# Gating products spread between the stages of a delta-rule attention loop

## Chip, cores and metric

The kernel runs on one core of a Trainium2 chip. The metric is the device time of one execution in microseconds. Lower is better. [...]

## The reference, cut to what matters

Three layers follow one another, all in float32, with B = 4, H = 8 heads of D = 48, S = 768, model width 384, inner width 1024:

```python
# 1: delta-rule attention, a recurrence over the 768 tokens of 32 (batch, head) units
k_n = k / (norm(k) + 1e-6)
for t in range(S):
    y[:, :, t] = einsum('bhd,bhde->bhe', q[:, :, t], state)
    v_old = einsum('bhde,bhd->bhe', state, kt)
    state = state + bt * einsum('bhd,bhe->bhde', kt, vt - v_old)
# 2: gating layer on x = y as (batch, token, 384)
h = gelu(x @ w_in);  u, v = h[..., :512], h[..., 512:]
v_n = layernorm(v) * g_ln
v_s = einsum('ts,bsd->btd', w_sg, v_n) + b_sg
x = x + (u * v_s) @ w_out
# 3: squared-relu layer with a shift by one token and a sigmoid gate
k = maximum(xk @ w_k, 0); out = sigmoid(xr @ w_r) * (k * k @ w_v)
```

## The kernel before, in words

The attention is done in chunks of 64 tokens: 12 chunks s, two of them a group g, six groups. In each chunk the 32 units fall into two halves o. Five stages make one chunk and half: st_rq (state times keys, and keys times keys and queries, into PSUM; then the sum `r` of line 466 on DVE, or of line 464 on ACT in group 0; then copies on ACT and masks on GpSimd), st_d (the solved 32 x 32 inverses times r; copied by ACT as u1), st_n (the coupling of a chunk's two 32-token blocks; copied by ACT), st_s (the state's update; copied) and st_y (the outputs; copied, and stored into xT by SP's queue). Each stage is a Python generator: its first piece issues the matmuls, the second the copies or the sum, the third, of st_rq alone, the negated copies and the masks. The matmuls of a stage are small (32 to 64 columns; lines 489, 492, 512, 525, 540, 554).

A group needs two things before its chunks: Gram blocks (`gram`, lines 328 and 330, eight halves of 32 pairs of weight load and matmul, in four jobs of two halves) and triangular inverses that `solver` makes on DVE in some hundred small steps over about a group's time; when they are there, `couple` (line 448, 64 pairs, called for k = 0 and 1) multiplies them on TensorE.

Meanwhile the gating layer is prepared. `fill(n)` issues the products x @ w_in of earlier tokens (lines 624 and 676) worth n, a 512-column product counting 1 and a 256-column one 0.5. Such products come in units of nine; each group of tokens brings 72. If none is ready, `fill` issues warming products on a zero tile (`keep_warm`, line 715) in their place. Before a gating unit ends, gelu on ACT must empty its PSUM bank. The weights come as float64 bit pairs: `narrow` turns a block into a rounded part and a rest with DVE, ACT and GpSimd, and `scratch` stores both to DRAM; these jobs are started by `tick`.

The order on TensorE, ACT, DVE and GpSimd is the order in which this Python code issues. The loop has 12 x 4 runs; `run` issues one slot's stages (st_n and st_rq in turn with st_d, st_s, st_y), and then three points (`tick`): at each, due calls of `after(n, f)` (n points later), DVE's background steps of a budget of 1.62 (1.05 times that in group 0), at some points a Gram block; and at the end `fill(n)`, where n comes from a planned slot of 5.315 us less the run's costs by the table COST, at 0.235 us for a product. `used` carries what was over or left. Eight runs, 24 points, are a group. From point 125 on, one step a point of `early_items` prepares the mixing of the second layer (`begin_early`: fetches of w_sg into `stw`, their splits, the ring of v). A DMA that is issued by `nc.sync` stands in SP's one queue; it waits there for what it reads or overwrites, and later ones behind it.

Behind the loop, x_split, the gating units of the last group, mixing products (line 935) and the splits of w_sg's second half are issued in turn, then projection and the third layer.

Of the kernel before, what the change touches and what calls it, by code (L numbers as in the profile page):

```python
# [7 lines left out]
F32 = mybir.dt.float32  # L8
# [9 lines left out]
DM = 384  # L18
FF = 1024
HF = 512  # L20
P = 128
# [10 lines left out]
SV = 60  # L32
B0 = 1.05
PRE = 0.8
GRAM0 = 17
SOLVE0 = 1
RUN = (3, 2, 3)
SUMS = (0,)
EVERY = 6
LATE = 100  # L40
PUT = 2
JLAG = 2
BUDGET = 1.62
SLOT = 5.315
GSTEP = 2
LAGC = 2
JS = 18
NT_ = (3, 3, 3)
LNW = 1
# [5 lines left out]
COST = dict(rq=1.05, d=0.8, n=0.8, s=0.85, y=1.1)  # L55
# [26 lines left out]
def fused_kernel(  # L82
# [17 lines left out]
    nc = tc.nc  # L100
# [87 lines left out]
    def scratch(dram, name, nblk, n, cw=CW, pool=stg):  # L188

        d = dp.tile([nblk, P, 2, n], F32, name=name + "_d")  # L190

        def job(i, j):
            parts = []
            yield from narrow(dram, i, j, None, None, cw, pool, parts=parts)

            def put():
                nc.sync.dma_start(out=d[i, :, :, j:j + cw], in_=parts[0])

            yield PUT, put

        return d[:, :, 0], d[:, :, 1], [lambda i=i, j=j: job(i, j) for i in range(nblk) for j in range(0, n, cw)]
# [38 lines left out]
    with ExitStack() as at:  # L240
# [112 lines left out]
        def solver(g):  # L353
# [46 lines left out]
            for dst in (0, 1):  # L400
                for p in range(2):
                    o = 16 * p
# [33 lines left out]
            DTs[g] = DT  # L436
            yield 1.14
            for k in range(2):
                after(LAGC + k, lambda k=k: couple(g, k))

        def couple(g, k):

            w = bank()[:].rearrange("p a (b c) -> p (a b) c", c=32)
            GL, DT, u0 = GLs[g], DTs[g], NPR * k
            for u in range(u0, u0 + NPR):
                for h in range(2):
                    r = 64 * (1 - h)
                    T.matmul(w[r:r + 32, u - u0, :], lhsT=GL[r + 32:r + 64, u, :],  # L448
                             rhs=DT[r + 32:r + 64, u, :], start=True, stop=True)
            for r in (64, 0):  # L450
                A.activation(GL[r:r + 32, u0:u0 + NPR], w[r:r + 32], AF.Copy)
            used[0] += 1.4
            joined.add(2 * g + k)

        def scale_v(s):
# [125 lines left out]

        units, grams, opened, owed, splits, used = [], [], [[], None], [0], [], [0]
        spent = [0, 0, 0]
        later, vstat, streams, point = [], {}, [], [0, 0]

        def after(n, f):
            later.append((point[0] + n, f))
# [164 lines left out]
                    running[:] = [r for r in running if r[1] is not e[1]]  # L754
            debt[0] = min(t, 0) * (point[1] > 0)

        running, debt = [], [0]
        jobs = in_jobs + jobs
        n_jobs = len(jobs)

# [61 lines left out]
        def tick():  # L822
            g, n = divmod(point[0], 24)
            point[1] = min(g, 1) + 1
            gg, nn = divmod(point[0] - GRAM0, 24)
            if nn == 0 and 0 <= gg and gg + 2 < NG:
                grams.extend(gram(gg + 2))
            if n == 0 and g + 1 < NG:
                streams.append([point[0] + SOLVE0, solver(g + 1), "solve"])
            late = point[0] >= LATE  # L830
            if point[0] < LASTP and jobs and len(running) < RUN[1 + late] and n % (2 if late else EVERY) == 0:
                start_job(LJ5 if late else LJ)
            background(BUDGET * (B0 if g == 0 else 1))
            while len(jobs) > n_rest and len(running) < RUN[0]:
                start_job()
            if grams and (point[0] - GRAM0) % GSTEP == 0:
                for _, f in grams.pop(0):
                    f()
                used[0] += 1.1
            point[0] += 1  # L840

        def run(*todo):
            bodies = [f(s, o) for f, s, o in todo]
            used[0] += sum(COST[f.__name__[3:]] for f, _, _ in todo)
            for _ in range(3):
                for b in bodies:
                    next(b, None)
            for _ in range(3):
                tick()
                if early_items and point[0] >= FROM:  # L850
                    early_items.pop(0)()
            n = min(max((SLOT - used[0]) / 0.235, 3), 14)
            used[0] += n * 0.235 - SLOT
            fill(n)

        ring, rb, wsl, early_items = {}, [], [[], []], []

# [13 lines left out]
        def begin_early():  # L871
            vst = [slot(G0[c + 1], [P, HF]) for c in range(4)]
            st = {0: fetch_pair(slot(W0[2], [P, 2, DM]), 0),
                  1: fetch_pair(stg.tile([P, 2, DM], F32, name="stw", bufs=1), 1)}
            for c in range(4):
                nc.sync.dma_start(out=vst[c], in_=vn_d[0, c])

            def ws(c):
                i, k = divmod(c, 2)
                if k == 0:  # L880
                    t = [slot(x, [P, 2, DM], F32R) for x in W0[2 * i:2 * i + 2]]
                    wsl[0].extend((t[0][:, e], t[1][:, e]) for e in range(2))
                split(A, V, st[i][:, k], *wsl[0][c])
                if c == 3:
                    st[2] = fetch_pair(stg.tile([P, 2, DM], F32, name="stw", bufs=1), 2)

            for x in (0, 1, 10, 2, 11, 3, 12, 13, 4, 5):
                early_items.append((lambda c=x: ws(c)) if x < 10 else
                                   (lambda c=x - 10: to_ring(0, c, vst[c])))

        for s in range(12):
# [297 lines left out]
```

## Time and profile before

| | us |
|---|---|
| median of three runs | 777.8 |
| lowest and highest of them | 776.1, 784.21 |
| the profiled execution, its own time | 785.01 |
| its span from first to last instruction | 783.3 |
| mean granted clock of TensorE in it | 0.961 |

The times of the rows below come from the profiled execution and are counted from the start of its span. The attention loop is the stretch from 56.8 to 345.9 us.

### The profile page before, as it was taken

What the parts mean: (1) busy time and instruction counts of PE and PEld (TensorE: products, weight loads), DVE (VectorE), ACT (ScalarE), POOL (GpSimd) and SP (SyncE); (2) the same over time, 40 slices, a digit from 0 to 9 for tenths busy, and PEclk for the clock granted to TensorE, in tenths of its full rate; (3) what the DMA queues carried; (4) which work ended last, traced back from release to release, by engine and by line L of the source; (5) the groups of instructions that cost most, each with busy time, mean ns of one, the idle gap of its engine ahead of it and who ended that gap; (6) DMA issues with size and microseconds to landing.
All of it is one profiled execution on the core that took longest, in us unless ns stands there. A gap on an engine that the chain in (4) does not pass through costs nothing.

```text
span 783.3 us, 25096 instructions
## 1 busy us (share of the span) xinstructions
PE 717.5 (92%) x10898; PEld 658.0 (84%) x10898; DVE 504.7 (64%) x1071; ACT 373.2 (48%) x752; POOL 199.9 (26%) x246
## 2 busy tenths in 40 slices
PE   3479989899998999798889979999999999999998
PEld 3335768788887887686879969999999999999997
DVE  6997779779597895622265967269664564564441
ACT  2234566566766767753333332128463463452330
POOL 3143335344363564520216351201000000000000
PEclk9979999899799999999989989999999999999999
DMA  8312346365566647538367554228000000000000
GB/s 240 79 62 67 112 94 190 104 187 168 130 175 175 189 142 199 180 106 223 122 228 237 180 163 146 75 87 222 21 11 31 11 21 31 11 21 31 11 22 31
DMA packets 82159, 88.76 MB, mean 113 GB/s; under 512 B 24704, under 2 KB 65024, under 8 KB 82048
## 3 DMA queue, kind: packets, MB, share of 16 engines
q1 hardware_dynamic: 76816, 77.92, 33.8%
q0 software_dynamic: 4800, 9.04, 4.2%
q8 instruction: 85, 1.39, 0.8%
q10 hardware_dynamic: 432, 0.20, 0.1%
q14 instruction: 26, 0.21, 0.1%
HBM read 56.60 MB, written 25.82 MB: 105 GB/s over the span
## 4 chain that ended last, share of the span: by engine, by line
PE 75%; DMA 7%; DVE 7%; issue 3%; POOL 3%; ACT 2%; SPq 2%; POOLq 0%; DVEq 0%
PE ms L146 35%; PE ms L676 7%; PE ms L935 6%; PE ms L624 6%; PE ms L715 4%; PE ms L554 3%; PE rk L512 3%; PE rk L489 2%; PE rk L525 2%; PE sps L540 2%; PE ms L448 2%; PE ms L328 2%; DVE sg L350 1%; DMA raw<-in_w_r_dram 1%; POOL na L172 1%
## 5 line engine op out<-in xcount | busy, mean ns | idle before, releaser
L146 PE MATMUL ms<-wvh,sl 128*128 128x384 f32 x192 | 64.6, 336 | 0.0
L146 PE MATMUL ms<-wvl,sh 128*128 128x384 f32 x192 | 64.5, 336 | 0.0
L146 PE MATMUL ms<-wvh,sh 128*128 128x384 f32 x192 | 64.5, 336 | 0.0
L146 PE MATMUL ms<-xm_hi,sw0h 128*128 128x384 f32 x192 | 64.2, 335 | 0.0
L146 PE MATMUL ms<-xm_hi,sw0l 128*128 128x384 f32 x192 | 64.2, 334 | 0.0
L146 PE MATMUL ms<-xm_lo,sw0h 128*128 128x384 f32 x192 | 64.2, 334 | 0.0
L172 POOL TENSOR_TENSOR na<-na,raw 128x256 int32<-128x256 int32 (+2 forms) x43 | 38.3, 890 | 86.1 <-DVE na L170 80.4
L118 DVE TENSOR_TENSOR sl<-sg,sh 128x384 fp32r<-128x384 f32 x64 | 35.6, 557 | 30.3 <-ACT sh L115 30.2
L935 PE MATMUL ms<-sw0h,g 128*128 128x384 f32 x192 | 50.4, 336 | 2.1 <-DVE g L118 2.1
L115 ACT ACTIVATE sh<-sg 128x384 fp32r<-128x384 f32 x64 | 33.5, 524 | 36.3 <-DVE sg L1109 36.3
L935 PE MATMUL ms<-ws1h,g 128*128 128x384 f32 x192 | 49.9, 334 | 0.0
L676 PE MATMUL ms<-xh,wiu_hi 128*128 128x256 f32 x144 | 41.0, 303 | 6.9 <-ACT v L633 6.9
L1125 DVE TENSOR_TENSOR sg<-sg,ms 128x384 f32<-128x384 f32 x24 | 13.3, 554 | 46.2 <-PE ms L146 46.2
L1109 DVE TENSOR_TENSOR sg<-sg 128x384 f32<-128x384 f32 x64 | 35.3, 552 | 11.5 <-ACT sg L1108 11.4
L350 DVE TENSOR_TENSOR sg<-sg,Yt 128x512 f32<-128x512 f32 (+10 forms) x78 | 41.5, 532 | 1.6
L1108 ACT ACTIVATE sg<-ms 128x384 f32<-128x384 f32 x64 | 30.8, 481 | 24.2 <-PE ms L146 23.9
L676 PE MATMUL ms<-xl,wiu_hi 128*128 128x256 f32 x144 | 40.0, 297 | 2.4 <-issue 2.4
L115 ACT ACTIVATE gh<-w 128x384 fp32r<-128x384 f32 x32 | 16.6, 524 | 53.5 <-DVE w L1022 53.5
L676 PE MATMUL ms<-xh,wiu_lo 128*128 128x256 f32 x144 | 40.4, 299 | 0.1
L146 PE MATMUL ms<-gh,wo_hi 128*128 128x384 f32 x96 | 35.2, 366 | 5.7 <-ACT gh L115 5.7
L505 POOL TENSOR_SCALAR_AFFINE_SELECT SQ<-SQ 64x512 f32<-64x512 f32 x36 | 26.9, 746 | 48.0 <-ACT SQ L504 41.1
L676 PEld LDWEIGHTS ms<-xh,wiu_hi 128*128 128x128 f32 x144 | 27.7, 201 | 13.1 <-ACT v L633 8.2
(236 smaller groups left out, 2244.9 us busy)
## 6 DMA issues: line engine op xcount, KB each, us to landing
u_d<-ug SPq DMA_DIRECT2D x24, 256.0 KB, 4.1
u<-u_d SPq DMA_DIRECT2D x16, 384.0 KB, 5.5
vn_d<-v SPq DMA_DIRECT2D x22, 256.0 KB, 3.8
vk<-in_vk_dram SPq DMA_DIRECT2D x24, 192.0 KB, 3.9
vk<-in_vk_dram SPq DMA_DIRECT2D x12, 384.0 KB, 4.9
out_dram<-sg SPq DMA_DIRECT2D x24, 192.0 KB, 1.9
SQ<-in_q_d_dram SPq DMA_DIRECT2D x36, 96.0 KB, 3.6
xT<-yst SPq DMA_DIRECT2D x23, 144.0 KB, 3.8
```

The costliest lines, as they stand in the source:

```text
L115: A.activation(hi, src, AF.Copy)
L118: eng_lo.tensor_tensor(lo, src, hi.bitcast(F32), op=ALU.subtract)
L146: T.matmul(pt, lhsT=a, rhs=b, start=(i == 0), stop=(i == n - 1))
L172: G.tensor_tensor(a.bitcast(I32), a.bitcast(I32), w_lo.bitcast(I32), op=ALU.add)
L350: V.tensor_tensor(tv, vw(a_t, a_off, a_dims), vw(b_t, b_off, b_dims), op=ALU.mult)
L505: G.affine_select(out=pt, in_=pt, pattern=[[0, 8], [1, C]], compare_op=ALU.is_gt, fill=0.0, base=0, channel_multiplier=-1)
L624: T.matmul(vstat[g, b], lhsT=a[:, c], rhs=w[:, c], start=first, stop=last)
L676: T.matmul(vstat["u"][:, 2 * P * d:2 * P * d + 2 * P], lhsT=w[:, c, ds_], rhs=a[:, c].rearrange("p b t -> p (b t)"), start=first, stop=last)
L715: T.matmul(o, lhsT=warm, rhs=vw(warm, 0, [(0, 4), (1, P)]), start=True, stop=True)
L935: T.matmul(pt[:, :DM], lhsT=v[:, ds_], rhs=w, start=(c == 0 and i == 0), stop=(c == 5 and i == 2))
L1108: A.activation(r, pt[:, :DM], AF.Relu)
L1109: V.tensor_tensor(r, r, r, op=ALU.mult)
```

## The change

The order in which TensorE gets its work inside the loop is made anew. `run` now issues for each stage its matmuls and its second piece and then a share of the run's products (`fill(gap)`); the third pieces, the points, and after them the calls in `batches`, each followed by another share. Gram blocks and couples go to `batches`: a block as two halves. Blocks stand at points 13, 18, 21 and 23 of a group (before: 17, 19, 21, 23), couples 2 and 8 points behind the solver's end (before: 2 and 3). The run's number of products is planned ahead: `need` counts the stages, 1.1 for each Gram point in the run and 1.4 for a run that begins at point 0 or 6, whether or not there is a block or couple; between 3 and 15 products (before 3 to 14), with at most 1 us carried on. The stores of rounded blocks (column width below 384: those of w_out and w_k, 20 of them) are issued by GpSimd in place of SP, one point after the split in place of two. Jobs start at points 0, 5, 10, 15, 20 of a group in place of 0, 6, 12, 18, and every second point from 110 on in place of 100. The third fetch of w_sg in `begin_early` is issued two points later, and the two splits that read it two points later.

```diff
@@ -32,18 +32,17 @@
 SV = 60
 B0 = 1.05
 PRE = 0.8
-GRAM0 = 17
+GRAMS = (13, 18, 21, 23)
 SOLVE0 = 1
 RUN = (3, 2, 3)
 SUMS = (0,)
-EVERY = 6
-LATE = 100
-PUT = 2
+EVERY = 5
+LATE = 110
+PUT = 1
 JLAG = 2
 BUDGET = 1.62
 SLOT = 5.315
-GSTEP = 2
-LAGC = 2
+LAGC = (2, 8)
 JS = 18
 NT_ = (3, 3, 3)
 LNW = 1
@@ -194,7 +193,7 @@
             yield from narrow(dram, i, j, None, None, cw, pool, parts=parts)
 
             def put():
-                nc.sync.dma_start(out=d[i, :, :, j:j + cw], in_=parts[0])
+                (G if cw < DM else nc.sync).dma_start(out=d[i, :, :, j:j + cw], in_=parts[0])
 
             yield PUT, put
 
@@ -436,7 +435,10 @@
             DTs[g] = DT
             yield 1.14
             for k in range(2):
-                after(LAGC + k, lambda k=k: couple(g, k))
+                after(LAGC[k], lambda k=k: join(g, k))
+
+        def join(g, k):
+            batches.append(lambda: couple(g, k))
 
         def couple(g, k):
 
@@ -449,7 +451,6 @@
                              rhs=DT[r + 32:r + 64, u, :], start=True, stop=True)
             for r in (64, 0):
                 A.activation(GL[r:r + 32, u0:u0 + NPR], w[r:r + 32], AF.Copy)
-            used[0] += 1.4
             joined.add(2 * g + k)
 
         def scale_v(s):
@@ -581,7 +582,7 @@
 
 
 
-        units, grams, opened, owed, splits, used = [], [], [[], None], [0], [], [0]
+        units, grams, opened, owed, splits, spare = [], [], [[], None], [0], [], [0]
         spent = [0, 0, 0]
         later, vstat, streams, point = [], {}, [], [0, 0]
 
@@ -754,7 +755,7 @@
                     running[:] = [r for r in running if r[1] is not e[1]]
             debt[0] = min(t, 0) * (point[1] > 0)
 
-        running, debt = [], [0]
+        running, debt, batches = [], [0], []
         jobs = in_jobs + jobs
         n_jobs = len(jobs)
 
@@ -822,7 +823,7 @@
         def tick():
             g, n = divmod(point[0], 24)
             point[1] = min(g, 1) + 1
-            gg, nn = divmod(point[0] - GRAM0, 24)
+            gg, nn = divmod(point[0] - GRAMS[0], 24)
             if nn == 0 and 0 <= gg and gg + 2 < NG:
                 grams.extend(gram(gg + 2))
             if n == 0 and g + 1 < NG:
@@ -833,25 +834,33 @@
             background(BUDGET * (B0 if g == 0 else 1))
             while len(jobs) > n_rest and len(running) < RUN[0]:
                 start_job()
-            if grams and (point[0] - GRAM0) % GSTEP == 0:
-                for _, f in grams.pop(0):
-                    f()
-                used[0] += 1.1
+            if grams and point[0] % 24 in GRAMS:
+                batches.extend(f for _, f in grams.pop(0))
             point[0] += 1
 
         def run(*todo):
-            bodies = [f(s, o) for f, s, o in todo]
-            used[0] += sum(COST[f.__name__[3:]] for f, _, _ in todo)
-            for _ in range(3):
-                for b in bodies:
-                    next(b, None)
+            n = point[0] % 24
+            plan = sum(k in GRAMS for k in range(n, n + 3)), n in (0, 6)
+            need = sum(COST[f.__name__[3:]] for f, _, _ in todo) + 1.1 * plan[0] + 1.4 * plan[1]
+            gap = min(max((SLOT - need + spare[0]) / 0.235, 3), 15)
+            spare[0] = min(spare[0] + SLOT - need - 0.235 * gap, 1)
+            gap /= len(todo) + 2 * plan[0] + plan[1] + (n < 3 and not todo)
+            bodies = []
+            for f, s, o in todo:
+                b = f(s, o)
+                next(b, None)
+                next(b, None)
+                bodies.append(b)
+                fill(gap)
+            for b in bodies:
+                next(b, None)
             for _ in range(3):
                 tick()
                 if early_items and point[0] >= FROM:
                     early_items.pop(0)()
-            n = min(max((SLOT - used[0]) / 0.235, 3), 14)
-            used[0] += n * 0.235 - SLOT
-            fill(n)
+            while batches:
+                batches.pop(0)()
+                fill(gap)
 
         ring, rb, wsl, early_items = {}, [], [[], []], []
 
@@ -882,10 +891,10 @@
                     wsl[0].extend((t[0][:, e], t[1][:, e]) for e in range(2))
                 split(A, V, st[i][:, k], *wsl[0][c])
                 if c == 3:
-                    st[2] = fetch_pair(stg.tile([P, 2, DM], F32, name="stw", bufs=1), 2)
-
-            for x in (0, 1, 10, 2, 11, 3, 12, 13, 4, 5):
-                early_items.append((lambda c=x: ws(c)) if x < 10 else
+                    after(2, lambda: st.update({2: fetch_pair(stg.tile([P, 2, DM], F32, name="stw", bufs=1), 2)}))
+
+            for x in (0, 1, 10, 2, 11, 3, 12, 13, 20, 20, 4, 5):
+                early_items.append((lambda c=x: ws(c)) if x < 10 else (lambda: None) if x == 20 else
                                    (lambda c=x - 10: to_ring(0, c, vst[c])))
 
         for s in range(12):
```

## Rows read from the trace of the kernel before

**Rows 1.** The page: busy share and instructions of each engine; instruction queue (packets, MB).

```profile
PE 717.5 (92%) x10898; PEld 658.0 (84%) x10898; DVE 504.7 (64%) x1071; ACT 373.2 (48%) x752; POOL 199.9 (26%) x246
...
q8 instruction: 85, 1.39, 0.8%
```

**Rows 2.** Windows, groups 0 to 5, behind: width, PE PEld DVE ACT POOL busy, clock, DMA.

```profile
56.80:96.70 39.90, 39.44 (x1078) 25.59 (x1077) 30.87 (x73) 20.27 (x45) 12.88 (x16) 1.00 0.28 84
96.70:148.40 51.70, 46.74 (x1377) 39.21 (x1376) 43.38 (x99) 33.18 (x66) 22.30 (x27) 0.93 0.51 136
148.40:198.80 50.40, 45.98 (x1390) 40.03 (x1388) 39.59 (x95) 33.95 (x67) 21.92 (x29) 0.97 0.58 162
198.80:249.80 51.00, 47.87 (x1390) 42.69 (x1389) 41.35 (x94) 33.79 (x67) 22.18 (x28) 0.90 0.59 165
249.80:296.30 46.50, 46.47 (x1163) 40.75 (x1162) 39.28 (x92) 31.58 (x60) 25.85 (x29) 0.93 0.58 162
296.30:345.90 49.60, 44.93 (x1115) 37.32 (x1114) 23.40 (x44) 34.91 (x68) 22.73 (x33) 0.93 0.58 166
345.90:400.00 54.10, 44.62 (x304) 41.05 (x303) 13.19 (x25) 18.83 (x32) 6.91 (x12) 0.97 0.62 173
```

**Rows 3.** Chain of waits in group 1, an even stretch: start us, us, what.

```profile
113.02 3.40 PE ms L624 x14
116.41 0.81 PE rk L512 x64
...
119.16 1.12 PE ms L624 x4
...
122.18 0.80 PE rk L525 x32
...
124.08 2.59 PE ms L676 x20
...
131.37 1.81 PE ms L624 x7
```

**Rows 4.** Chain of waits in groups 4 and 5: a couple, warming products.

```profile
260.64 1.13 PE ms L448 x64
...
300.14 2.05 PE ms L715 x9
```

**Rows 5.** Chain of waits in groups 1 and 3: pauses and what stands around.

```profile
98.34 0.46 issue
...
99.48 1.70 PE ms L448 x100
101.18 2.27 issue
...
138.38 3.29 PE ms L624 x7
...
246.84 2.41 issue
```

**Rows 6.** Windows, a stretch of half clock; columns as in rows 2.

```profile
199.80:210.00 10.20, 10.20 (x304) 9.59 (x301) 7.71 (x34) 6.53 (x13) 3.64 (x8) 0.50 0.39 107
```

**Rows 7.** Timeline of TensorE, group 5 and behind: start, us, line, [idle before, releaser].

```profile
330.20 1.98 PE L554 MATMUL ms<-SQ 128*64 128x64 f32 x32 [2.52 <-ACT ug L680]
...
364.36 0.96 PE L624 MATMUL ms<-wiv_hi,xh 128*128 128x512 f32 x3 [0.48 <-ACT xh L115]
...
371.96 0.61 PE L676 MATMUL ms<-xh,wiu_hi 128*128 128x256 f32 x3 [3.22 <-ACT v L633]
```

**Rows 8.** Waits of SP's queue, whole span: us in total, times, longest.

```profile
SPq L197 <- POOL raw L118: 72.9, 22, 8.7
```

**Rows 9.** Timeline of DVE in group 1: start, us, line.

```profile
125.33 0.54 DVE L466 TENSOR_TENSOR r<-vk,rk 128x384 f32<-128x384 f32 x1
```

**Rows 10.** Issues of DMAs by GpSimd, two lines: ns min/median/max, first and last start.

```profile
L207 POOL DMA_DIRECT2D wo_hi<-wo_d x1: 1003/1003/1003, 349.6 to 349.6; - x1
...
L1064 POOL DMA_DIRECT2D sw0l<-wk_d x3: 537/537/650, 501.9 to 516.6; - x3
```

## Prediction

> **What bounds the kernel now.** I read first the page's busy shares, then a table of windows with one row for each group of the attention loop, then the chain of waits, piece by piece, inside that loop. TensorE is busy 92% of the span [rows 1]. The loop (56.8 to 345.9 us, six groups of eight runs) takes 289.1 us [rows 2], and in it nearly every piece of the chain is a TensorE piece that begins where the last one ended. So the loop lasts as long as what is put on TensorE's queue, plus the places where that queue stops or runs slowly.
>
> What a group should take follows from pieces in an undisturbed stretch [rows 3]: 14 gating products take 3.40 us (0.243 each), st_d, st_s and st_y together 2.75 us (116.41 to 119.16), st_n 0.80 and st_rq 1.10 (122.98 to 124.08), and one Gram block (64 pairs of weight load and matmul) 1.02 us, the time from the end of st_y at 130.34 to the first product at 131.37. A couple takes 1.13 us [rows 4]. Eight runs are 4 x 1.90 + 4 x 2.75 = 18.6; four Gram blocks 4.1; two couples 2.3; and the planner's 72 products 17.5: together 42.5 us. Groups 1, 2 and 3 took 51.7, 50.4 and 51.0 [rows 2], 25.6 us more in all.
>
> Where that goes can be read off. **Stops**: at 98.34, 101.18 and 246.84 TensorE stands still for 0.46, 2.27 and 2.41 us and the chain calls it "issue", so nothing that the profile shows held it [rows 5]. Between the first two stops the engine ran the last 27 pairs of st_rq and 100 of the couple, 127 pairs. One instruction transfer carries 256 instructions (2 x 10898 instructions in 85 transfers [rows 1]), which is 128 pairs: the stops sit where such a block ends. They come in or just behind long strings of small matmuls (Gram, couples). The loop has nine "issue" stops over 0.4 us, from 82.20 to 246.84, three of them shown: 0.42, 0.46, 2.27, 1.98, 1.14, 0.63, 1.19, 0.72 and 2.41, together 11.2 us. [...]
>
> **The change part by part.** (1) *Spreading.* No pair is added or taken away: a Gram block becomes two halves of 32 pairs with products behind each, and products stand behind each stage instead of at the run's end. The two couples of a group, which fell into one run in groups 1 to 3, are six points apart; one of four Gram blocks moves from the run at point 15 to the one at 12. But the run at point 21 keeps two blocks behind st_d, st_s, st_y, 256 small pairs with the least number of products, 3, among them. Price per block when the queue is dry: from 98.80 to 103.45, 4.65 us for 128 pairs, the upper bound; the lower bound is that a block costs nothing beyond its own matmuls. In the three runs from point 18 to point 2 the kernel before issues about 656 pairs in 16 us by plan; less one block of lead, 528 / 128 x 4.65 = 19.2, so 3.2 us of stop per group (seen: 3 to 5). With a couple less it is some 596 pairs: 17.0, so 1.0 us per group. I take 4 us of stops left of 11.2, and about a quarter of the half clock, 3 of 12.2 us: a gain of 16. [...] The first run has 15 warming products where it had 10, some 1 us more.
>
> (2) *Number of products.* Both planners' arithmetic (5.315 less the stages' costs, over 0.235) gives the same total through group 3, 306 and 304. After it the new one charges Gram blocks at points 13, 18, 21 and 23 of groups 4 and 5, where there are none, and drops their share of the products: 180 planned before, 120 after. 60 x 0.243 = 14.6 us leave TensorE's loop. 19 of these were warming products, as the one row of nine shows [rows 4] with two more of five: pure gain, 4.6 us. The other 41 are real and move behind the loop. There they meet the time up to 364.36, when the last group's last block comes to its products [rows 7], already filled with mixing, and three pauses, of which the first, 3.22 us, is shown [rows 7], with 2.25 and 0.67 behind it, in which banks wait for gelus on ACT. I take it that 3 us of their 10 are absorbed: +7 behind the loop (bounds 0 and 10).
>
> (3) *What is late next.* DVE is busy 43.4, 39.6, 41.4 and 39.3 us in groups 1 to 4 [rows 2], with a rounding more per group now (5 starts in 24 points, not 4), for which I allow up to 2 us. TensorE's 42.5 is thus just where DVE ends as well, and in group 4, where TensorE would need only 34 (18.6 + 2.3 + 53 x 0.243), DVE sets the end. In group 5 it is ACT, 34.9 us. So I take 45.5, 44, 44.5, 41.5 and 41.5 for groups 1 to 5 and 39.5 for group 0: 256.5 against 289.1. These values hold the gains of (1) and (2) inside the loop, capped by the other engines; for half clock that the caps' own short waits bring back I add 3.
>
> (4) *Less cover behind st_rq.* Its sum on DVE (line 466) must be there before st_d of the next run. Before, all products of the run, 3.4 us, lay between; now a half of them, with a couple or Gram block in groups 0 to 3 some 2.2 to 2.9 us, but in four runs of groups 4 and 5 only 2.5 products, 0.6 us. The sum takes 0.54 us and started as late as 1.25 us after the products it reads ended at 124.08 [rows 9]. So 18 runs hide it, four wait up to 1.3 us: at most 5 us, in groups that other engines bound anyway; nothing added.
>
> (5) *Stores by GpSimd.* 20 stores of rounded blocks leave SP's queue. SP stood 72.9 us for GpSimd's last step of such blocks, up to 8.7 at a time [rows 8], with loads of keys and queries and stores of gating results queued behind. In group 5 a gelu on ACT, whose buffer waits for such a store, made st_y wait 2.52 [rows 7]; that wait and the half clock after it should go (in group 5's 41.5). On GpSimd each issue costs 0.54 to 1.0 us by its issues behind the loop [rows 10], 11 to 20 us over a loop in which it was busy 128 of 289 us [rows 2]; queued behind are the roundings' sums, on which ACT waits, and st_rq's masks, needed three runs later. I take nothing for it and up to 5 us in the range.
>
> (6) *Third gating fetch two points later, its splits two steps later, late roundings from 110, stores one point earlier*: SP no longer stands for that fetch's buffer; at most 2 us either way, taken as nothing.
>
> The sum is made on the profiled execution (785.0 us, span 783.3): 289.1 - 256.5 = 32.6, less 3 of returned half clock, less 7 behind the loop: 22.6, so 762. The runs' median is 777.8, and 22.6 from that gives 755. Part of the 7 us between the two must be stops and half clock that the change takes away in either case; I take the middle, **758 us**.
>
> **The rivals.** *Blocks still run dry.* At 21 to 24 points four blocks' worth of small pairs remain with few products. If a refill costs the 4.65 us throughout and half of the half clock stays, (1) brings 8 instead of 16: 767. For: three products do not fill 256 pairs. Against: neighbours are now lighter.
>
> *The stops are no refills.* Then they have a cause that the order of the products does not touch, a pause of TensorE's own queue that comes wherever the long strings stand, and they and the half clock stay. Only the 19 warming products, the wait of 2.52 and 3 us of clock around it are gained, 4.6 + 2.5 + 3, so 768. The distance of 127 pairs between two stops [rows 5] speaks against it; that a stop in group 3 [rows 5] falls among products and not in a string speaks for it. [...]
>
> *All of it comes through.* Postponed products fit wholly into the pauses and the other engines follow: 7 + 3 more, 745 to 748.
>
> *DVE late for st_d (slower than before).* If DVE, with no slack left, runs behind by over 1.7 us at each of the 22 sums, the cover of (4) is gone in every run: 22 waits of 1.2 us are 26 us, TensorE falls to half clock in their wake (5 us), and the postponed products (10) come without relief: 41 against a gain of 32.6, 786. It decides from about 1 us of wait per run on. For: groups at 95 to 100% DVE. Against: at 125.33 the sum, 1.25 late, ended at 125.87 [rows 9], 1.6 us before 14 products behind st_rq would (124.08 + 3.4).
>
> **How the numbers follow.** Forecast 0.5 (750 to 766), blocks still dry 0.18, no refills 0.1, all of it 0.14, DVE late 0.08. A measurement of this kernel tells about 1% (the runs lie from 776.1 to 784.2). Faster by over 1% (under 770): forecast, all of it and most of the two at 767 and 768, 0.78; within 1% 0.14; slower 0.08. The range that leaves out no more than 2 in 10 reaches from 743 to 775.
>
> **What would show it.** Right: groups 1 to 3 near 44.5 us, "issue" in the chain under 5 us of the loop, granted clock 0.97 or more in each group, DVE over 90% busy in groups 1 to 4, no SP wait for a store of a rounded block in the loop, three warming rows at the end of group 4 gone; some 41 products more behind the loop and that part 5 to 10 us longer. Wrong: stops unchanged in length at the same kinds of place (then the refill's price or cause was wrong); TensorE waiting at st_d for DVE in most runs; a tail longer by over 10 us; or st_y waiting for masks that GpSimd makes late behind its stores.

## The result, and the profile after

The changed kernel takes **784.8 us** (median of 20 runs, 779.94 to 790.98) against 778.82 of the kernel before beside it (20 runs, 773.92 to 785.17): 1.0077, interval 1.0049 to 1.0104. It is 0.8% slower; 758 had been forecast. Ratios, here and below, leave out executions more than 1.5% longer than a kernel's shortest.

The two profiled executions rank the other way round: that of after took 779.94 us, its shortest of the 20, and that of before 785.01, longer than all but one of its 20. So a difference between the two traces is no part of the 6 us by itself. I use the traces for prices (what one thing costs, at equal work and clock), and runs for the sum.

The page of after, busy shares and the instruction queue, answers to [rows 1]: 13 matmuls fewer and the same 85 transfers of instructions, so the work is the same.

```profile
PE 714.5 (92%) x10885; PEld 639.3 (82%) x10885; DVE 512.9 (66%) x1071; ACT 371.7 (48%) x752; POOL 210.3 (27%) x266
...
q8 instruction: 85, 1.39, 0.7%
```

Windows of after by group, from the first st_d to the end of the last st_y, and behind it up to the projection; columns as in [rows 2]. Then the last group of before to the same point, and behind it.

```profile
57.11:95.84 38.73, 38.27 (x1068) 24.10 (x1067) 32.37 (x75) 20.38 (x44) 13.04 (x17) 1.00 0.31 87
95.84:147.45 51.61, 48.08 (x1376) 35.88 (x1370) 43.83 (x97) 32.65 (x64) 22.91 (x30) 0.97 0.49 137
147.45:197.40 49.95, 48.08 (x1391) 38.75 (x1389) 40.85 (x96) 33.85 (x68) 27.25 (x34) 1.00 0.58 163
197.40:248.13 50.73, 47.91 (x1391) 38.71 (x1389) 44.26 (x95) 32.89 (x64) 25.72 (x32) 1.00 0.59 167
248.13:293.44 45.31, 42.01 (x1129) 34.77 (x1122) 38.89 (x89) 30.33 (x59) 24.96 (x32) 0.96 0.60 159
293.44:345.72 52.28, 45.03 (x1166) 36.82 (x1165) 25.32 (x45) 37.26 (x72) 24.07 (x34) 0.97 0.54 147
...
345.72:396.70 50.98, 47.59 (x287) 44.58 (x287) 13.39 (x26) 18.15 (x32) 8.12 (x16) 1.00 0.66 192
...
296.30:349.12 52.82, 47.27 (x1180) 39.33 (x1179) 23.96 (x45) 37.00 (x72) 22.73 (x33) 0.94 0.58 162
...
349.12:398.80 49.68, 41.25 (x234) 38.26 (x234) 11.43 (x22) 16.32 (x28) 6.91 (x12) 0.97 0.61 173
```

The loop took 288.6 us; before, measured to the same point (the last st_y ends at 349.12, behind the end of [rows 2]), 292.3. Groups 1 to 3 stand at 51.6, 50.0 and 50.7 where 45.5, 44 and 44.5 were forecast. Look at group 2: clock 1.00 throughout, TensorE busy 48.08 of 49.95 us. So no stop and no clock explains it: the matmuls themselves take 48 us where the prediction's sum was 42.5.

The chain of waits of after, in pieces: start us, us, what. The first five are products between small matmuls, the last two stops.

```profile
114.25 0.89 PE ms L625 x3
...
115.95 1.12 PE ms L625 x4
...
138.68 0.66 PE ms L625 x2
...
140.16 0.42 PE ms L625
...
142.05 1.41 issue
...
243.37 2.40 issue
```

One product alone takes 0.42 us, two 0.66, three 0.89, four 1.12: 0.23 for each and **0.19 for the string as such**. [Rows 3] hold the same line: 14 in 3.40 and 7 in 1.81 give 0.227 for each and 0.22 over. The prediction had divided 3.40 by 14.

TensorE's waits in the loop of after: what waited, for what, us in all, times, longest.

```profile
PE rk L513 <- DVE r L467: 5.4, 2, 3.9
PE ms L327 <- issue: 3.3, 3, 2.4
PE ms L677 <- issue: 2.3, 2, 1.5
PE ms L555 <- issue: 2.0, 2, 1.4
```

All "issue" waits together are 10.7 us (14 of over 0.1 us); before, counted alike, 11.6. The wait of st_y for the gelu's bank, 2.52 in [rows 7], is gone; waits of st_d for DVE's sum have come.

### The profile page after: what moved, and what is told of

Its sections match the earlier page's. It is cut to its first block, busy times and chain, and to the rows that moved or that the text cites. A ratio compares the mean times of both kernels' runs of the same rounds, so it can differ in the third digit from the quotient of the medians.

```text
span 778.2 us, 25068 instructions
## 1 busy us (share of the span) xinstructions
PE 714.5 (92%) x10885; PEld 639.3 (82%) x10885; DVE 512.9 (66%) x1071; ACT 371.7 (48%) x752; POOL 210.3 (27%) x266
## 4 chain that ended last, share of the span: by engine, by line
PE 70%; DVE 11%; DMA 7%; issue 4%; POOL 3%; ACT 3%; SPq 1%; POOLq 0%; ACTq 0%; DVEq 0%
PE ms L145 34%; PE ms L625 6%; PE ms L944 5%; PE ms L677 5%; PE ms L555 3%; PE ms L716 3%; PE rk L513 2%; PE sps L541 2%; DVE sg L349 2%; PE rk L526 2%; PE ms L450 2%; PE rk L490 2%; DMA stw<-in_w_sg_dram 2%; PE ms L327 2%; POOL na L171 1%
## 5 line engine op out<-in xcount | busy, mean ns | idle before, releaser
L349 DVE TENSOR_TENSOR sg<-sg,Yt 128x512 f32<-128x512 f32 (+10 forms) x78 | 44.9, 576 | 1.8
L1118 DVE TENSOR_TENSOR sg<-sg 128x384 f32<-128x384 f32 x64 | 35.3, 552 | 11.5 <-ACT sg L1117 11.4
L677 PE MATMUL ms<-xh,wiu_hi 128*128 128x256 f32 x144 | 37.9, 295 | 3.0 <-ACT v L634 3.0
L677 PE MATMUL ms<-xh,wiu_lo 128*128 128x256 f32 x144 | 38.4, 299 | 2.3 <-issue 2.3
L114 ACT ACTIVATE xm_hi<-sg 128x384 fp32r<-128x384 f32 x48 | 23.4, 517 | 31.7 <-PE ms L145 30.5
L145 PE MATMUL ms<-gh,wo_hi 128*128 128x384 f32 x96 | 33.0, 344 | 5.1 <-ACT gh L114 5.1
L677 PE MATMUL ms<-xl,wiu_hi 128*128 128x256 f32 x144 | 37.5, 292 | 0.0
L163 DVE TENSOR_SCALAR na<-raw 128x256 uint32<-128x256 uint32 (+2 forms) x43 | 20.9, 486 | 24.5 <-DMA raw<-in_w_v_dram 14.0
```

The source lines that it names most:

```text
L114: A.activation(hi, src, AF.Copy)
L145: T.matmul(pt, lhsT=a, rhs=b, start=(i == 0), stop=(i == n - 1))
L349: V.tensor_tensor(tv, vw(a_t, a_off, a_dims), vw(b_t, b_off, b_dims), op=ALU.mult)
L677: T.matmul(vstat["u"][:, 2 * P * d:2 * P * d + 2 * P], lhsT=w[:, c, ds_], rhs=a[:, c].rearrange("p b t -> p (b t)"), start=first, stop=last)
L1118: V.tensor_tensor(r, r, r, op=ALU.mult)
```

## The experiments

Ratios are to runs of the kernel before on the same chip, with 95% intervals. "Chunk" means a string of products with small matmuls before and after it. The loop of before has 47 chunks (one a run), after has 143; in groups 2 and 3 it is 8 against 26 each.

**One part or the other.** First the spreading with its planning alone (after, with the small edits undone), and the small edits alone (on before):

```diff
# spread_only, against after
-EVERY = 5
-LATE = 110
-PUT = 1
+EVERY = 6
+LATE = 100
+PUT = 2
-(G if cw < DM else nc.sync).dma_start(out=d[i, :, :, j:j + cw], in_=parts[0])
+nc.sync.dma_start(out=d[i, :, :, j:j + cw], in_=parts[0])
-after(2, lambda: st.update({2: fetch_pair(...)}))
+st[2] = fetch_pair(...)
# and no item 20 in the list of early items; rest_only: these lines of after, on before
```

> The changed kernel's order on TensorE alone (products behind each stage, Gram halves, couples six points apart, planned products); stores by SP, third fetch, starts of roundings as before. Theory A (every chunk of products between small matmuls costs about 0.2 us, and there are 144 in place of 47 in the loop): about as slow as the changed kernel, 782 to 788 us where the kernel before takes 779; the trace shows some 140 chunks. Theory B (the stores by GpSimd and the denser roundings are what costs): faster than the kernel before, 770 to 775.

> The kernel before with only the other edits: stores by GpSimd, third fetch two points later, roundings every 5 points and from 110 on. Theory A: the same as the kernel before or up to 4 us less (SP's waits gone), 775 to 779. Theory B: 6 us or more slower than before, 785 to 790.

Spreading alone: 1.0165 (1.0117 to 1.0212), 795.4 us. The small edits alone: 1.0093 (1.006 to 1.0127). Each alone is slower than the two together, so they are not a sum. Spreading alone lost its time in group 5, 63.7 us; the timeline of TensorE there shows st_d behind DVE:

```profile
338.54 1.51 PE L513 MATMUL rk<-r,DT 32*32 32x48 f32 x64 [9.82 <-DVE r L467]
```

**How often products are cut.** After, with the products of the stages in one chunk behind the last stage; and with all products of a run in one chunk at its end.

```diff
# one_chunk_stages
     bodies.append(b)
-    fill(gap)
 ...
+fill(gap * len(todo))
# one_chunk_run, instead
+k = len(todo) + len(batches)
 while batches:
     batches.pop(0)()
-    fill(gap)
+fill(gap * k)
```

> The changed kernel, but the products that it puts behind each stage of a run stand in one chunk behind the last stage; those behind Gram halves and couples stay. Some 85 chunks. Theory A: 60 chunks fewer at 0.2 us are 12 us, so 772 to 777 us. Theory C (what costs is that products are dropped in groups 4 and 5 and st_d waits for the sum on DVE): as the changed kernel, 782 to 787.

> The changed kernel with all products of a run in one chunk at its end, behind the Gram halves and couples too; points of Gram blocks, couples and the number of products as changed. Some 48 chunks. Theory A: 19 us less than the changed kernel for the chunks, of which longer strings of small matmuls take back 5 to 10 in stops and half clock: 768 to 777. Theory C: as the changed kernel, 782 to 787.

1.0102 (1.0052 to 1.0153) and 0.9964 (0.9914 to 1.0014). The first gained nothing as a whole (TensorE waited 12.5 us for DVE in its profile). The second is not to be told from before; its 12 executions spread from 772.6 to 794.7, and their median of 783.8 is above the 781.3 of before beside it, so its ratio says little.

**Each small edit.** Stores by GpSimd alone, and roundings every 5 points, late ones from 110, stores a point earlier alone, both on before:

```diff
# gpsimd_stores
-nc.sync.dma_start(out=d[i, :, :, j:j + cw], in_=parts[0])
+(G if cw < DM else nc.sync).dma_start(out=d[i, :, :, j:j + cw], in_=parts[0])
# denser_roundings
-EVERY = 6
-LATE = 100
-PUT = 2
+EVERY = 5
+LATE = 110
+PUT = 1
```

> The kernel before with only the stores of rounded blocks issued by GpSimd. The other edits together made the kernel before slower by 0.9%. Theory S (the stores cost: GpSimd's own work waits behind them, or their transfers disturb others): 0.6 to 1.0% slower than before. Theory R (the denser roundings cost): no change, or up to 0.4% faster, since SP's waits go.

> The kernel before with only the starts of roundings every 5 points and from 110 on, stores one point after the split (by SP). Theory R (DVE, which is 80 to 90% busy in groups 1 to 4, gets a rounding more per group and holds up the solver and the sums): 0.6 to 1.0% slower than before. Theory S: no change within 0.3%.

1.009 (1.0052 to 1.0128) and 1.0033 (0.9995 to 1.007). So on before the stores alone cost what all small edits cost. SP's waits in the loop of gpsimd_stores:

```profile
SPq L155 <- DMA wo_d<-raw: 33.2, 8, 7.7
SPq L155 <- DMA wk_d<-raw: 28.4, 5, 9.2
```

SP no longer stands at the store (in the loop of before 39.8 of the 72.9 us of [rows 8]). It stands at the next load of the same buffer, which must wait until the store has read it, 61.6 us where before these two rows were 7.0 and 4.4. Loads of keys queue behind it, and a Gram block waited 2.36 us for them. That is a part of the 7 us that the stores cost; what makes up the rest is not shown.

```profile
248.37 0.27 PE L328 MATMUL ms<-kT 64*32 64x64 f32 x2 [2.36 <-DMA kT<-in_kt_d_dram]
```

**The dropped products given back.** After, with Gram points and couples counted only where there are some:

```diff
-plan = sum(k in GRAMS for k in range(n, n + 3)), n in (0, 6)
+plan = ((point[0] < 96) * sum(k in GRAMS for k in range(n, n + 3)),
+        n in (0, 6) and point[0] != 6)
```

> The changed kernel, with Gram blocks and couples charged to a run only where there are any, so that groups 4 and 5 keep their products. Theory C (the dropped products lay bare the waits of st_d for the sum on DVE, 5.4 us in the changed kernel's profile, and a stretch of half clock behind): 4 to 8 us less than the changed kernel, 777 to 781. Theory A alone (chunks cost, dropped products do not): 784 to 788, since some 13 more chunks stand in the loop.

1.0137 (1.0092 to 1.0183), no faster than the change at 1.0077 (to 1.0104): the smaller number of products is not what it lost by, and more likely a gain in it.

**The switch by itself.** Behind the loop of before, 96 products and 768 small pairs (64x32 by 64x64), cut in 24 and in 6, and both once more. Only the times of this stretch count; its results go nowhere.

```python
for _ in range(24):
    products(4)
    pairs(32)
for _ in range(6):
    products(16)
    pairs(128)
```

> The kernel before with an addition behind the loop whose results nobody reads: 24 times 4 gating products and 32 small pairs, then 6 times 16 products and 128 pairs, and both once more. The same work, with 18 switches to products more in the finer one. Theory A (about 0.2 us for each switch): the finer pattern is 3.0 to 4.5 us longer. If a switch costs nothing beyond its matmuls: under 0.5 us.

Windows of these four stretches, then pieces of the chain:

```profile
355.64:407.00 51.36, 51.36 (x866) 38.27 (x864) 1.92 (x2) 3.70 (x5) 1.76 (x2) 1.00 0.28 72
407.00:452.50 45.50, 45.50 (x869) 39.17 (x865) 0.00 (x0) 0.00 (x0) 0.00 (x0) 1.00 0.01 2
452.50:503.88 51.38, 51.38 (x869) 38.30 (x865) 0.00 (x0) 0.00 (x0) 0.00 (x0) 1.00 0.01 2
503.88:549.40 45.52, 45.52 (x869) 39.19 (x865) 0.00 (x0) 0.00 (x0) 0.00 (x0) 1.00 0.01 3
```

```profile
355.71 1.12 PE ms L909 x4
356.84 0.17 PE ms L914
...
407.07 3.87 PE ms L909 x16
```

5.86 us for 18 chunks more: 0.325 us each, at clock 1.00, busy throughout and with no transfers in the later stretches. 4 products take 1.12 and 16 take 3.87, so 0.229 each and 0.20 on top; the first small piece behind products (L914) takes 0.17 where later ones take 0.05, 0.12 more.

**Is it the stores or the fetch in the whole?** After with the stores back on SP; spread_only with the third fetch later; one_chunk_run with the stores on SP; and the kernel before again, for a second profile.

> The changed kernel with the stores of rounded blocks back on SP's queue; everything else of the change stays. On the kernel before, these stores by GpSimd cost 0.9%. If that price is GpSimd's own time for the issues and SP's waits moved to the next load, it is the same here, and this kernel comes to 0.998 to 1.001 of the kernel before, some 778 us. Rival: the price hung on the old order (the load of keys that came late there), and with products spread the stores' place does not matter: 1.006 to 1.01, some 785 us. Loop by the first 283 to 286 us, by the second 288 to 291.

> The spread order with only the third fetch of w_sg and its splits later, all of the other small edits undone (spread alone stood at 1.0165, with 63.7 us in group 5 and a wait of 9.8 us of st_d for DVE). If the fetch that comes too early is what DVE stands behind in group 5, that group falls to 52 to 55 us, the wait to under 5 us, and the whole to 1.000 to 1.006 (less than the changed kernel, as the stores are back on SP). Rival: the fewer or later roundings of the other edits freed DVE there; then group 5 stays above 60 us and the whole at 1.013 to 1.02.

> The changed kernel with all products of a run in one chunk at its end, and the stores of rounded blocks by SP. With one chunk a run, the changed kernel stood at 0.9964. If chunks and stores cost separately, this comes to 0.986 to 0.990, some 770 us, and beats both kernels. Rival: the stores cost only where they meet the old planning; then 0.994 to 0.999.

> The kernel before once more, unchanged, for a second profile of it: the first one was of one of its longest executions. Both theories expect its loop's stops to come to 9 to 13 us again, and half clock in the loop to between 20 and 35 us; were these two under 6 and 10 us, the stops would belong to that one execution and not to the kernel.

sync_stores 1.0079 (1.0052 to 1.0107): the rival holds, in the new order the stores' place costs nothing. spread_third 1.0142 (1.0103 to 1.0182), group 5 at 60.5 us: my theory of the third fetch falls. What separates it from sync_stores is only the rhythm of the roundings and their earlier stores; with these, 1.0142 becomes 1.0079. one_chunk_run_sync 1.0015 (0.9989 to 1.0042): no better than before, and above both of its forecasts. before_again: 780.84 us, loop 290.3 us, stops 10.4, so the first profile's stops were no accident.

sync_stores and one_chunk_run_sync are one kernel with its products cut and whole, run side by side: 785.9 and 780.6 us by median, so the cuts cost 5 us on balance. Windows of the two loops, cut and whole, show what is paid and what is got for it:

```profile
56.91:348.62 291.71, 272.37 (x7499) 210.67 (x7498) 227.28 (x494) 187.69 (x370) 124.73 (x158) 0.97 0.52 144
57.44:346.38 288.94, 258.80 (x7499) 216.19 (x7498) 218.53 (x486) 187.11 (x368) 122.36 (x158) 0.95 0.52 146
```

With 7499 matmuls in each and 143 against 49 chunks, TensorE is busy 13.6 us longer in the cut one. Its half clock, as twice (1 - clock), is 10 us shorter (mean clock 0.971 against 0.953), 4.6 us less lost at 45% (seven products took 3.29 us at half clock [rows 5], 1.81 at full [rows 3]), so at full clock the 94 chunks cost 18.2 us, 0.19 each. In return its "issue" stops are 5.8 us in place of 16.9. The cuts thus cost a little more than the stops and the clock give back.

Single groups give the same price. Windows of group 2, clock 1.00 in all four, 72 products, 1388 or 1389 weight loads. One chunk a run (8 in the group), one_chunk_run_sync and then strings_apart (below):

```profile
147.47:198.93 51.46, 44.72 (x1389) 39.03 (x1389) 41.26 (x96) 34.25 (x69) 23.06 (x30) 1.00 0.59 163
```

```profile
146.03:194.74 48.71, 44.62 (x1389) 38.77 (x1388) 41.94 (x95) 33.30 (x67) 21.63 (x29) 1.00 0.63 169
```

one_chunk_stages, 15 chunks; after, with 26, stands above (48.08):

```profile
144.64:196.03 51.39, 46.30 (x1393) 39.09 (x1389) 41.19 (x96) 33.92 (x68) 28.10 (x35) 1.00 0.58 162
```

44.7, 46.3 and 48.1 us of TensorE for 8, 15 and 26 chunks: 3.4 us for 18, 0.19 each.

**What the stops are.** Three strings of 1024 small pairs behind the loop of before, eight instruction blocks each; from 64 products before the second on, ten copies of 1 MB within DRAM. Only the times of the strings count.

```python
pairs(1024); 64 products
for c in range(10):
    nc.sync.dma_start(out=x_d[c % 4, 0:4], in_=vn_d[c % 4, 0:4])
products(64); pairs(1024); products(64); pairs(1024)
```

> The kernel before with three strings of 1024 small pairs (64x32 by 64x64, 8 instruction blocks each) behind its attention loop, 64 products before the second and the third; from the first 64 products on, copies of 1 MB each from DRAM to DRAM run beside them. So its time is longer by the strings; only the strings are read. A pair that follows a pair takes 0.0288 us (128 in 3.69), so a string without stops takes 29.5 us. If the stops in the loop are refills that get late behind other transfers, the first string shows stops of at most 0.5 us a block (30 to 33 us in all), and a string with copies beside it 1 to 3 us a block, 37 to 53 us in all. If a dry queue costs 4.65 us a block always, as the prediction had it, all three take 37 us. If the stops are no refills, all three take 29.5 us.

Windows of the three strings, and of the piece between two stops of the first one:

```profile
351.13:384.94 33.81, 30.67 (x1024) 30.26 (x1024) 1.91 (x2) 3.69 (x5) 1.76 (x2) 0.95 0.49 150
414.25:446.07 31.82, 29.36 (x1025) 28.70 (x1024) 0.00 (x0) 0.00 (x0) 0.00 (x0) 1.00 0.25 76
460.91:489.55 28.64, 28.64 (x1025) 28.55 (x1024) 0.00 (x0) 0.00 (x0) 0.00 (x0) 1.00 0.02 4
...
361.00:365.00 4.00, 1.27 (x30) 1.11 (x26) 0.00 (x0) 0.00 (x0) 0.00 (x0) 0.88 1.01 299
...
420.00:423.50 3.50, 1.04 (x38) 0.88 (x33) 0.00 (x0) 0.00 (x0) 0.00 (x0) 1.00 0.88 222
...
357.51:361.27 3.76, 3.76 (x128) 3.60 (x128) 0.00 (x0) 0.81 (x1) 0.00 (x0) 1.00 0.63 177
```

The chain in the same stretch has three stops:

```profile
357.10 0.41 issue
...
361.27 2.73 issue
...
420.23 2.46 issue
```

The third string, beside no transfers, crosses eight blocks without a stop, 28.64 / 8 = 3.58 us a block. Two stops of the first have exactly 128 pairs between them, one block. The long ones, 2.73 and 2.46, fall where the transfers' share is 1.01 and 0.88.

The traces also tell what a stop is. Counted through the records of TensorE (matmuls and weight loads), the 25 "issue" stops of over 0.1 us in the loops of before and after stand a multiple of 256 records apart, less about one for each 256 (from the first stop to the last 36 x 256 less 35 in before, 46 x 256 less 42 in after): each is a block's end, the one among products at 246.84 [rows 5] too. Of the three stops here the second comes 128 matmuls behind the first and the third 1024 behind the second (687 small ones, 128 products, 209 small ones), one block and eight. And in each of the 25 TensorE went on 0.9 to 1.7 us after a transfer of the instruction queue q8 had ended, which itself took 0.9 to 1.6 us. In the longest of after and of before, 2.40 us at 243.37 and 2.41 at 246.84, that transfer began only when TensorE already stood still, 0.01 and 0.07 us into the stop. So I read the stops as refills that come late.

The sizes I had expected were off: the copies had nearly ended when the second string met its first block's end (so 31.8 us, not 37), and the kernel's own transfers ran beside the first.

**Strings apart without cutting.** Before with Gram blocks at 13, 18, 21, 23 and couples 2 and 8 behind the solver; the same with the third fetch later; before with the counts of absent Gram blocks in groups 4 and 5; strings apart with these.

```diff
# strings_apart
-    after(LAGC + k, lambda k=k: couple(g, k))
+    after(LAGC[k], lambda k=k: couple(g, k))
-if grams and (point[0] - GRAM0) % GSTEP == 0:
+if grams and point[0] % 24 in GRAMS:
# fewer_products (with the points 17, 19, 21, 23) and strings_apart_fewer (with GRAMS)
+if not grams and point[0] > 96 and point[0] % 24 in GRAMS:
+    used[0] += 1.1
```

> The kernel before, with only the small strings further apart: Gram blocks at points 13, 18, 21 and 23 (whole, where points issued them before), the two couples 2 and 8 points behind the solver in place of 2 and 3. The products stay in one chunk a run, so no switch is added. If the price of the change was its switches, this has the spreading's gain without it: stops in the loop down to 6 to 9 us, half clock by 5 to 15 us, 0.990 to 0.996. Rival: what makes a stop is one block's own pairs and the transfers beside it, wherever the strings stand; then stops stay at 10 to 12 us and the ratio at 0.998 to 1.002.

> The same, with the third fetch of w_sg and its splits two points later as in the change. If that fetch and its splits hold DVE and SP in group 5, this is 0.2 to 0.4% below the one without it; rival: nothing, as group 5 is bound by ACT there.

> The kernel before, with the second part of the change alone: at the eight Gram points of groups 4 and 5, where there are no blocks, the planner counts 1.1 us each all the same, so up to 37 products fewer are issued there (8.8 us over 0.235); order, chunks and all else are the kernel before. The prediction's step: products leave the loop, warming ones for good and the real ones into pauses behind it, so 0.990 to 0.995. First rival: the real ones come back behind the loop at full cost and only warming is gained, 0.997 to 0.999. Second rival: DVE and ACT end groups 4 and 5 anyway, so what leaves TensorE's queue there turns into waits, the real ones come on top behind the loop: 1.003 to 1.008.

> The kernel before with the small strings apart (that alone: 0.9974) and the fewer products of groups 4 and 5. If the two add up and the fewer products gain, 0.988 to 0.993, faster than both kernels beyond doubt; if the products come back behind the loop, 0.995 to 0.998; if groups 4 and 5 wait for DVE and ACT instead, 1.000 to 1.004.

0.9974 (0.9943 to 1.0004), 0.9982 (0.9952 to 1.0012), 0.9985 (0.9958 to 1.0013) and **0.9925 (0.9893 to 0.9958)**, 772.9 us. The first three are not told from before by themselves; the third fetch adds nothing. The last is faster than before by 0.7%, and so than after. Its trace does not say that this is the stops' doing: 14.1 us of them in its profiled execution, 6.8 in that of strings_apart, which was one of its shortest. fewer_products shows in groups 4 and 5 what leaves and what comes back:

```profile
247.79:290.23 42.44, 42.44 (x1134) 37.55 (x1133) 36.02 (x88) 29.37 (x55) 23.10 (x28) 0.92 0.57 158
290.23:347.13 56.90, 48.67 (x1190) 42.75 (x1189) 26.58 (x49) 38.18 (x74) 25.06 (x35) 0.91 0.57 161
```

Group 4 is 4 us shorter than in [rows 2]; group 5, 56.9 against 52.8 to the end of its last st_y, gives that back, with a wait of 4.0 us of the couple for the solver on DVE in it.

## Why the prediction was wrong, step by step

**The failed step is the first of part (1), with part (2) and the group sums standing on it**: "no pair is added or taken away", hence each product 0.243 us wherever it stands. A chunk costs some 0.19 us of its own between small matmuls. The loop has 96 more of them: 18 us, two thirds of the 27 between 758 and 784.8. The small side's 0.12 us hardly counts here, since stages that follow one another pay it too: in the chain of before st_rq, right behind st_n, begins with the long piece.

```profile
122.98 0.18 PE rk L489
123.20 0.04 PE rk L489 x2
```

The account of the two profiled loops comes out with that price. The granted clock in the two traces is 0.50 or 1.00 in every stretch on record, so half clock, as twice (1 - clock) of each window, is 33 us before (windows to 349.12) and 10 after; at a loss of 45% that is 15.0 and 4.4 us. TensorE was busy 273.7 and 269.4 us, so 258.7 and 265.0 at full clock, though 18 warming products (0.23 each) and 34 real ones, 11.9 us, had left the loop. 265.0 + 11.9 - 258.7 = 18.2 us, or 0.19 for each of 96 chunks. Against it stand 10.6 us of clock, 11.9 of products and 0.9 of stops; other waits rose by 1.5. That leaves the 3.7 us of difference between the loops.

**Stops** (part 1): 4 us forecast, 10.7 found. In the profiles of the five kernels with the whole spread order (after, sync_stores, spread_only, spread_third, charge_real) they are 5.8 to 10.7 us, in six with the order and strings of before 10.4 to 15.4: cutting shortened them, by less than forecast. The price of 4.65 us for a block in a dry queue was wrong: it made one block's stop of 2.27 us the price of every block. In dry_blocks a block of 128 pairs alone took 3.58 us without a stop; beside transfers three ends of such blocks cost 0.41, 2.46 and 2.73, others nothing. A group's 1389 pairs in 50 us are a block every 4.6 us at DMA shares of 0.5 to 0.6. The traces show that the refill of the longest stops begins late (0.01 and 0.07 us into them), and dry_blocks that its two long stops fell together with transfers (shares of 1.01 and 0.88); what makes a refill late is not shown. The one block of lead in the forecast's count of stops was an assumption that no run tests. Of the rivals "the stops are no refills" falls, since all 25 stand at block ends, the stop among products that spoke for it too. "Blocks still run dry" was right that many stops stay, but its 767 leaves out the chunks.

**Half clock** (part 1): right in this profile. The 12.2 us of loss in the forecast's sum is shown by no run: the windows of before give 33 us of half clock and with it 15.0. The 3 and 5 us of half clock that new waits were to bring were estimates. The 45% comes from the seven products at 138.38 [rows 5], beside the seven at 131.37 [rows 3]; this is the clock around the slow ones:

```profile
138.30:141.70 3.40, 3.40 (x12) 2.73 (x10) 3.40 (x8) 1.10 (x4) 1.90 (x2) 0.50 0.29 107
```

A loss of 9 us was to go and 10.6 went, 4.4 are left; groups 2 and 3 have none. Of an ordinary execution that is too much: in sync_stores, at the same ratio, 17 us of half clock are left, a loss of 7.7.

**Fewer products** (part 2): 34 real and 18 warming products left the loop, 41 and 19 were forecast. Behind it, up to the projection, 287 matmuls stand where before 234 stood, but the stretch grew only from 49.7 to 51.0 us, so +1.3 for a forecast of +7: TensorE's idle time there fell from 8.4 to 3.4 us. Right in direction, and charge_real speaks for its having paid.

**DVE and ACT late next** (part 3): not the bound. DVE was busy 82 to 87% of groups 1 to 4, for a forecast of over 90.

**Less cover behind st_rq** (part 4): "nothing added" was wrong: 5.4 us of waits came, just over the bound of 5, and they were two waits, not four small ones. The timeline of DVE shows the longer one's cause:

```profile
321.10 1.74 DVE L117 TENSOR_TENSOR sw0l<-stw,sw0h 128x384 fp32r<-128x384 f32 x1 [5.68 <-ACT sw0h L114]
...
325.45 0.69 DVE L117 TENSOR_TENSOR g<-sg,g 128x512 fp32r<-128x512 f32 x1 [0.70 <-ACT g L114]
326.06 0.55 DVE L467 TENSOR_TENSOR r<-vk,rk 128x384 f32<-128x384 f32 x1
```

DVE stood 5.68 us for a step of w_sg's split on ACT, and the sum stood behind it in order. So the rival "DVE late" came about in two places of groups 4 and 5, and in the orders without the denser roundings with waits of up to 9.8 (spread_only) and 5.9 us (spread_third). It was not the lag at each of the 22 sums that I had priced.

**Stores by GpSimd** (part 5): "SP freed" was wrong: of the 72.9 us in [rows 8] only 39.8 fell in the loop, and that wait moved to the next load of `raw` (32.2 and 23.9 us in after). The 0.68 to 0.87 us of an issue on GpSimd were within the bounds. Costing it at nothing came out right only in the new order.

**What stays open.** The runs put the change at +6 us, the account above at -3.7 in the loop, since the profile of after is of its best execution. sync_stores, at the same ratio, had a loop of 291.7 us with 58.4 in group 5 in its profile, and before_again 290.3, so a usual execution of after may lose there. The granted clocks of all executions on record say the same: the two profiled ones, at 0.977 and 0.961, differ by 11 us of loss over the whole program, but the 20 of after, at 0.971 in the mean, lose only 6 us less than 110 of before, at 0.962. That takes some 5 us off the account's gain, and the stretch behind the loop adds 1.3, so the account comes to some +3 of the 6 us. The rest stays open. Why the small edits cost 0.9% on before and help on the spread order is shown only in part (the order of DVE's and ACT's work in group 5).

## What to carry to other kernels

Price a kind of matmul from two string lengths, not from the mean of a long string: slope and intercept lie in the same rows (here 0.23 and 0.19 us), and each of the 94 chunks that sync_stores has more than one_chunk_run_sync cost the intercept, 0.19 us. The only order that was clearly faster than the kernel before kept its products whole, moved the strings of small matmuls apart and planned fewer products in the last groups; it is 0.7% faster, and which wait it shortened is not shown. Before a store moves to another queue, look what the next load into its buffer waits for: in the loop of gpsimd_stores SP stood 61.6 us at such loads (11.4 in before), where the store had held it 39.8.

## What the runs showed of the hardware that was not expected

In switch_cost a change from small matmuls to 512-column products and back cost 0.20 and 0.12 us at clock 1.00, with the engine counted as busy all the while (51.36 of 51.36 us), so no idle row shows it. In dry_blocks eight blocks of 256 TensorE instructions passed in 3.58 us each without a stop beside transfers of a share of 0.02; at two block ends where transfers took 0.88 and 1.01 of the DMA engines' time TensorE stood still for 2.46 and 2.73 us. The 25 pauses of over 0.1 us that the profile calls "issue" in the loops of before and after began at block ends, and TensorE went on 0.9 to 1.7 us after the refill's transfer had ended.
